# Keys of an attention unit in three chunks of 128 and a shared rest of 64, for every unit instead of for the later ones

## The chip, the cores and the metric

The kernel runs on one core of a Trainium2 chip. The metric is the device time of one execution in microseconds (us); a comparison goes by the median of several. The engines of the core work side by side, each through its own instructions in the order of the program: TensorE (PE; its weight loads are listed as PEld), VectorE (DVE), ScalarE (ACT), GpSimd (POOL) and SyncE (SP). SP and POOL issue the DMA transfers here, and 16 DMA engines carry them out.

## What is computed

The reference is softmax attention, followed by a two-layer network with a leaky ReLU between the layers:

```python
attn = exp(q @ k.T / sqrt(64)); attn /= attn.sum(-1)      # 8 batches, 12 heads, 448 rows, 64 wide
x = (attn @ v).transpose(0, 2, 1, 3).reshape(3584, 768)
h = x @ w_in                                              # 768 x 2048
out = maximum(0.01 * h, h) @ w_out                        # 2048 x 768, float32
```

## The kernel before

**Units.** Attention is worked on in 48 units `u`: batch `u // 6`, and two of its heads. In a unit, `scores(u, c)` (L306) multiplies one chunk of keys by all 448 queries into a PSUM slot, `expo(u, c)` (L321) takes the exponential of it on ACT, `pv` (L361) or `rows` (L857) multiplies the exponentials by the values and by a column of ones, and DVE divides by the sum that the ones give (L873, L874). `x_transposes` (L374) turns the result into `xT`, where the features lie on partitions, on PE (L384) or as a DMA transpose that SP issues (L269).

**Two forms of a unit.** For `u < HY = 18` (batches 0 to 2) the 448 keys are four chunks of 112: eight score matmuls (two heads that lie in the two halves of the partitions), four exponentials of 112x896, and 32 matmuls of 65 columns in `pairs` (L350). For the other 30 units they are three chunks of 128, and the last 64 keys of the two heads share one block of 128 partitions: seven score matmuls, three exponentials of 128x896 and one of 128x448, and in `weighted` (L333) four matmuls of 130 columns and 24 of 65.

**Loads.** `load_soft` (L147) is issued by POOL and casts to bf16 on the way, a transfer for each of q, k, v and each two units; k and v of a later unit take two transfers (L154 to L160). POOL then copies ("casts", L177) each unit's piece into `qkb` (q and k) and `v_old` or `v_sb`; in a later unit the rest of 64 takes two more small copies each for k (L189, L190) and v (L196, L197). q and k are transposed into `qkT` on PE up to unit 14 (L287, `NPE = 15`), then by DMA (L271).

**Order of the work.** The schedule is manual: each engine's order is that of the program. First (L799) come units 0 to 5, one `first(u)` (L761) each, with the casts and loads of later units in `supply(u)` (L749) at hand-set places. `head` (L683) then computes the first layer for the first 448 tokens, `neck` (L702) for the tokens to 640, which belong to batch 1, so it reads `xT` of units 6 to 11. Into these, `place` (L968) puts attention: bursts of three score chunks (L885), `tail` (L901, the score chunk of a rest), transposes, and `rows`, by a small table of assumed durations (`model`, L966) and by the goals `early` and `goals` (L1067); with each burst of head and neck `feed` (L938) issues casts, loads and weight loads. Then `second(i)` (L1031) computes the second layer of token range `i`, with more units placed between the products, and `hidden(i)` (L512) the first layer of the next range, without bursts. `plan` (L965) counts the bursts of each range.

**Stores.** `xT` is a ring of `NX = 15 * 128` tokens (L103). `v_old` lies in the room of `x_mix`, `e_old` in that of the `c` tiles.

Of the kernel before, what the change touches and what calls it, by code (L numbers as in the profile page):

```python
# [16 lines left out]
def kernel(  # L17
# [64 lines left out]
    HY = 3 * HP  # L82
    v_all = v_pool.tile([P, NV, 2 * KC + 2, D + 1], BF16, name="v")
    v_sb = [v_all[:, i] for i in range(NV)]

# [6 lines left out]
    e_old = [c_pool.tile([P, 4 * P], F32, name="c").bitcast(BF16)[:, :2 * S + EP] for _ in range(NE)]  # L92
# [3 lines left out]
    qkT_all = qk_pool.tile([P, NQ, 2, NSC, P], BF16, name="qkT")  # L96
    qkT = [qkT_all[:, i] for i in range(NQ)]
    NB = 3
    qkb_all = cast_pool.tile([P, NB, 2, NSC, 2, D], BF16, name="qkb")
# [3 lines left out]
    NX = 15 * P  # L103

    def place_of(t):
        return (t + NX - cuts[3]) % NX

    OVER = -cuts[3] % S
# [14 lines left out]
    v_old = x_mix.rearrange("p x k n -> p (x k n)")[:SC, :NV * 2 * NSC * (D + 1)].rearrange(  # L123
        "p (u h so d) -> p u h so d", u=NV, h=2, so=NSC)
# [15 lines left out]
    def room(x, new):  # L140

        n = P if x and new else SC
        if not rooms:
            return ld_pool.tile([n, 2, NSC, D], F32, name="f" + "qkv"[x])
        return rooms.pop(0)[:n].bitcast(F32).rearrange("p (h so d) -> p h so d", h=2, so=NSC)

    def load_soft(u, n, which):  # L147
        b, hp = divmod(u, HP)
        hs = slice(2 * hp, 2 * hp + 2 * n)
        for x in which:  # L150
            new = x > 0 and u >= HY
            t = room(x, new).rearrange("p h so d -> p (h so d)").bitcast(BF16)
            t = t.rearrange("p (u h so d) -> p u h so d", u=2, h=2, so=NSC)
            for p, so, keys in ((slice(0, D), NSC, slice(0, NSC * D)), (slice(D, P), KC, slice(NSC * D, S))) if new else (  # L154
                (slice(0, SC), NSC, slice(0, S)),
            ):
                nc.gpsimd.dma_start(  # L157
                    out=t[p, :n, :, :so].rearrange("p u h so d -> p (u h) (so d)"),
                    in_=(q, k, v)[x][b, hs, keys].rearrange("h (p so) d -> p h (so d)", so=so),
                )  # L160
            for i in range(n):
                raw.setdefault(u + i, {})[x] = t[:, i]

    def load_one(u, x, queue):
        b, hp = divmod(u, HP)
        t = room(x, False)
        queue.dma_start(
            out=t.rearrange("p h so d -> p h (so d)"),
            in_=(q, k, v)[x][b, 2 * hp:2 * hp + 2].rearrange("h (p so) d -> p h (so d)", so=NSC),
        )  # L170
        raw.setdefault(u, {})[x] = t

# [4 lines left out]
    def cast(u, parts=(0, 1, 2), by=nc.gpsimd.tensor_copy):  # L177
        if u >= NU:
            return
        for x in parts:  # L180
            f = raw[u].pop(x)
            t = qkb[u % NB]
            if x < 2 and (x == 0 or u < HY):
                by(t[:SC, x].rearrange("p so h d -> p h so d"), f)  # L184
            elif x == 1:
                if u < HY + NB:
                    nc.gpsimd.memset(t[:, 1, KC], 0.0)
                by(t[:, 1, :KC].rearrange("p so h d -> p h so d"), f[:, :, :KC])
                by(t[:D, 1, KC, 0], f[:D, 0, KC])  # L189
                by(t[D:, 1, KC, 1], f[:D, 1, KC])  # L190
            elif u < HY:
                by(v_old[:, u % NV, :, :, :D], f)
            else:
                t = v_sb[u % NV]
                by(t[:, :2 * KC, :D].rearrange("p (h so) d -> p h so d", h=2), f[:, :, :KC])
                by(t[:D, 2 * KC, :D], f[:D, 0, KC])  # L196
                by(t[D:, 2 * KC + 1, :D], f[:D, 1, KC])  # L197
# [17 lines left out]
    make_identity(nc, ident)  # L215
    load_soft(1, 1, (0,))
    load_soft(2, 2, (0, 1))
    load_soft(0, 1, (2,))
    load_soft(1, 2, (2,))
# [5 lines left out]
    warm = h_mix.rearrange("p m c t -> p (m c t)")[:, :512]  # L225
    nc.vector.memset(warm, 0.0)

    gate = const_pool.tile([P, 2], F32)
    nc.vector.memset(gate, 0.0)
# [13 lines left out]
    nc.vector.memset(qkT_all.rearrange("p u i c s -> p u (i c s)")[:, :, 2 * S:2 * S + EP], 0.0)  # L243
    nc.vector.memset(v_old.rearrange("p u h so d -> p (u h so) d")[:, :, D:], 1.0)
    nc.vector.memset(e_all[:SC, :, EM:EM + EP], 0.0)
    for t in e_old:
        nc.vector.memset(t[:SC, 2 * S:], 0.0)
    nc.vector.memset(qkb_all.rearrange("p u i so h d -> p u i (so h d)")[3 * P // 4:, :, 0], 0.0)
    nc.vector.memset(v_all.rearrange("p u c d -> p u (c d)")[:, :, 2 * KC * (D + 1):], 0.0)
    nc.vector.memset(v_all[:, :, :2 * KC, D:], 1.0)  # L250
    for j in range(2):
        nc.vector.memset(v_all[j * D:(j + 1) * D, :, 2 * KC + j, D:], 1.0)
# [17 lines left out]

    def dma_transposes(u):  # L271
        if NPE <= u < HY:
            turn(
                qkT[u % NQ].rearrange("p i c s -> p (i c s)")[:, :2 * S],
                qkb[u % NB][:SC].rearrange("p i so h d -> p (i so h d)"),
            )
        elif NPE <= u < NU:
            nc.sync.dma_start_transpose(
                out=qkT[u % NQ].rearrange("p i c s -> p (i c) s"),
# [850 lines left out]
```

## Time and profile before

| what | us |
|---|---|
| median of 3 runs (382.24 to 384.49) | 382.76 |
| the profiled execution: its span, the one time recorded for it | 381.0 |
| median above that span | 1.8 |
| units 0 to 5, from the first exponential to unit 6's | 7.2 to 26.8 |
| units 6 to 13 with the first layer (head and neck) | about 26.8 to 73.8 |
| second layer of range 0, with its share of units | 73.8 to 105.1 |
| the six further ranges | 105.1 to 381.0 |

The page of the profile gives the busy time of each engine over the span, rows of digits for 40 slices of 9.5 us (9 is busy for 90% or more), groups of instructions with their mean duration, and the chain of work that ended last. The timeline lists instructions by start and duration, in us; rows of a queue (SPq) or rows with DMA are issues, and the trace has for each DMA its issue and its landing. A table by stretches gives busy us of each engine in parts of the span.

### The profile page before, as it was taken

How to read it: one execution, taken by the hardware profiler on the slowest of the kernel's cores; microseconds unless marked ns; L12 is line 12 of the kernel's file. 1: busy time of each engine (PE TensorE's matmuls, PEld its weight loads, DVE VectorE, ACT ScalarE, POOL GpSimd, SP SyncE). 2: the span in 40 equal slices, each digit the busy share in tenths (PEclk: the TensorE clock that was granted, in tenths of full speed). 3: DMA queues.
4: the chain of work that ended last, by engine and by line, in shares of the span. 5: the costliest groups of instructions: out<-in, count | busy, mean ns of one | idle time of the engine just before them, and what ended most of it. 6: DMA issues, size and time to landing. Idle time of an engine off the chain costs nothing.

```text
span 381.0 us, 9888 instructions
## 1 busy us (share of the span) xinstructions
PE 373.0 (98%) x3944; PEld 262.3 (69%) x3944; DVE 229.9 (60%) x488; ACT 254.9 (67%) x391; POOL 183.7 (48%) x376
## 2 busy tenths in 40 slices
PE   7899999999999999999999999999999999999996
PEld 3665657766598656886658866588665895668854
DVE  5663847445766646566476573765736665474753
ACT  5998885765848876478764878638787388617700
POOL 8988820996979456760576603848027100000000
PEclk9999999999999999999999999999999999999999
DMA  9999999699999759991499915999139800330022
GB/s 159 200 201 203 180 191 181 90 170 203 144 168 157 101 102 161 206 129 28 87 172 197 145 28 67 174 202 146 25 68 192 147 14 2 80 109 29 2 82 85
DMA packets 99294, 47.84 MB, mean 126 GB/s; under 512 B 63664, under 2 KB 95920, under 8 KB 99248
## 3 DMA queue, kind: packets, MB, share of 16 engines
q0 software_dynamic: 40384, 22.47, 47.9%
q1 hardware_dynamic: 58608, 24.52, 33.0%
q8 instruction: 31, 0.51, 0.5%
q10 hardware_dynamic: 256, 0.22, 0.2%
q14 instruction: 15, 0.12, 0.1%
HBM read 45.61 MB, written 11.01 MB: 149 GB/s over the span
## 4 chain that ended last, share of the span: by engine, by line
PE 93%; ACT 4%; DMA 1%; issue 1%; DVE 0%; ACTq 0%; DVEq 0%
PE g L609 32%; PE g L537 14%; PE sc L537 14%; PE sc L317 7%; PE sc L345 6%; PE g L419 4%; PE sc L314 4%; PE sc L357 3%; PE g L674 3%; ACT e L326 3%; PE g L715 2%; PE sc L338 2%; PE g L296 1%; DMA w_in_mix<-in_k_dram 1%; PE g L357 1%; ACT c L329 1%
## 5 line engine op out<-in xcount | busy, mean ns | idle before, releaser
L326 ACT ACTIVATE e<-sc 128x896 bf16<-128x896 f32 (+1 forms) x144 | 123.9, 930 | 34.0 <-PE sc L317 20.4
L609 PEld LDWEIGHTS <-h 128*128 128x128 bf16 x632 | 59.3, 98 | 44.7 <-issue 9.3
L609 PE MATMUL g<-w_out_sb,h 128*128 128x384 bf16 x416 | 78.7, 326 | 0.0
L184 POOL COPY qkb<-fq 112x512 bf16<-112x512 bf16 x36 | 24.0, 665 | 90.7 <-DMA qkT<-qkb 74.9
L526 ACT ACTIVATE h<-c 128x512 bf16<-128x512 f32 (+1 forms) x72 | 43.5, 611 | 25.2 <-DVE c L552 15.8
L537 PEld LDWEIGHTS <-w_in_sb 128*128 128x128 bf16 x576 | 54.3, 98 | 5.9
L537 PEld LDWEIGHTS <-w_in_mix 128*128 128x128 bf16 x432 | 41.2, 98 | 4.1
L873 DVE RECIPROCAL rec<-sc 112x8 f32<-112x8 f32 x42 | 8.7, 207 | 54.2 <-PE sc L345 25.9
L609 PE MATMUL g<-w_mix,h 128*128 128x384 bf16 (+1 forms) x208 | 39.0, 323 | 0.0
L614 DVE COPY o<-g 128x384 f32<-128x384 f32 x49 | 27.1, 552 | 10.4 <-PE g L609 10.1
L345 PE MATMUL sc<-v,e 128*128 128x65 bf16 x720 | 33.3, 193 | 0.0
L317 PE MATMUL sc<-qkT 64*128 64x448 bf16 (+1 forms) x210 | 32.8, 352 | 0.0
L345 PEld LDWEIGHTS <-e 128*128 128x128 bf16 x720 | 31.1, 98 | 1.4
L617 DVE TENSOR_TENSOR o<-o,g 128x384 f32<-128x384 f32 x39 | 21.6, 554 | 16.3 <-PE g L609 15.3
L874 DVE TENSOR_TENSOR x<-sc,rec 112x512 bf16<-112x512 f32 x42 | 29.0, 691 | 1.5
L537 PE MATMUL sc<-xT,w_in_sb 128*128 128x256 bf16 (+1 forms) x216 | 28.5, 268 | 0.0
L537 PE MATMUL g<-xT,w_in_sb 128*128 128x256 bf16 (+1 forms) x216 | 28.5, 268 | 0.0
L549 ACT COPY c<-g 128x512 f32<-128x512 f32 (+1 forms) x12 | 6.8, 569 | 30.8 <-PE g L537 30.8
L338 PE MATMUL sc<-v,e 128*128 128x130 bf16 x120 | 26.5, 220 | 0.0
L157 POOL DMA_DIRECT2D fv<-in_v_dram x33 | 20.6, 631 | 4.1 <-POOL v L197 2.4
L314 PE MATMUL sc<-qkT 64*128 64x448 bf16 x144 | 19.9, 357 | 2.1 <-ACT e L326 1.0
L357 PEld LDWEIGHTS <-e 112*128 112x128 bf16 x432 | 20.0, 98 | 1.8 <-issue 0.4
(131 smaller groups left out, 684.0 us busy)
## 6 DMA issues: line engine op xcount, KB each, us to landing
fq<-in_q_dram POOLq DMA_DIRECT2D x18, 224.0 KB, 5.9
w_in_sb<-in_moe_w_in_dram POOLq DMA_DIRECT2D x4, 768.0 KB, 11.2
w_out_sb<-in_moe_w_out_dram POOLq DMA_DIRECT2D x4, 768.0 KB, 19.5
out_dram<-o SPq DMA_DIRECT2D x7, 336.0 KB, 3.4
out_dram<-o SPq DMA_DIRECT2D x8, 288.0 KB, 4.0
fk<-in_k_dram POOLq DMA_DIRECT2D x15, 128.0 KB, 5.7
fv<-in_v_dram POOLq DMA_DIRECT2D x15, 128.0 KB, 4.1
out_dram<-o SPq DMA_DIRECT2D x7, 240.0 KB, 3.4
```

The costliest lines, as they stand in the source:

```text
L184: by(t[:SC, x].rearrange("p so h d -> p h so d"), f)
L314: nc.tensor.matmul(ps[:, j, :S], t[p, S + c * SC:S + c * SC + P], t[p, :S], start=True, stop=True)
L317: nc.tensor.matmul(ps[:, j, :S].rearrange("p (so s) -> p so s", so=NSC), t[p, 1, c], t[p, 0, :, :SC], start=True, stop=True,)
L326: nc.scalar.activation(e[:, :, c, :], ps[:n, :, :S], AX.Exp, scale=scale)
L338: nc.tensor.matmul(ps, e[:, EM + qc * SC:EM + qc * SC + P], vt[:, 2 * KC:].rearrange("p j d -> p (j d)"), start=True, stop=False, skip_gro ...
L345: nc.tensor.matmul(ps[:, j * (D + 1):(j + 1) * (D + 1)], e[:, at:at + P], vt[:, j * KC + c], start=False, stop=(c == KC - 1), skip_group_c ...
L357: nc.tensor.matmul(ps[:, qc, :], t[:SC, at:at + P], vt[:, c], start=(c == 0), stop=(c == NSC - 1),)
L526: nc.scalar.activation(hs[:, m:m + 2, cols], x.rearrange("p (m t) -> p m t", m=2), AX.Prelu, alpha=0.01)
L537: nc.tensor.matmul(ps[:, j * nh:(j + 1) * nh], w[:, kk, ts(j, P)], x[:, kk], start=(first and j == 0 and kk == 0), stop=(kk == KH - 1), sk ...
L609: nc.tensor.matmul(ps[:, cols], x[:, m], w[:, m], start=(first and m == 0), stop=(m == MH - 1), skip_group_check=True,)
L614: by(o[:, at], ps[:, :NW])
L874: nc.vector.tensor_mul(x, ps[:, :, :, :D], rec.to_broadcast([SC, 2, 2 * NP, D]))
```

## The change

All 48 units take the form with three chunks and a rest. The rests of k and of v are no longer loaded with the units: `load_rest(b, x)` loads those of a whole batch (12 heads, 64 keys) in two transfers, one for each half of the partitions, straight into a block-wise store whose other blocks hold zeros. There is room for two batches. The rests of k are transposed on PE with each unit's other pieces for batch 0, and for later batches by one DMA transpose of six blocks on SP, `turn_rest(b)`. `feed` and `advance` call `rests()`, which issues these when units are far enough. The main part is cut like this:

```diff
+    v_rest = v_pool.tile([P, 2, HP, 2, D + 1], BF16, name="vr")
+    k_rest = qk_pool.tile([P, 2, HP, 2, D], BF16, name="kr")
+    kT_rest = qk_pool.tile([P, 2, HP, P], BF16, name="krT")
-    NX = 15 * P
+    NX = 12 * P
...
+    def load_rest(b, x):
+        t = (None, k_rest, v_rest)[x]
+        for j in range(2):
+            nc.gpsimd.dma_start(
+                out=t[j * D:(j + 1) * D, b % 2, :, j, :D],
+                in_=(q, k, v)[x][b, j::2, KS:].rearrange("h p d -> p h d"),
+            )
...
+    nc.vector.memset(k_rest.rearrange("p b u h d -> p (b u h d)"), 0.0)
+    nc.vector.memset(v_rest.rearrange("p b u j d -> p (b u j d)"), 0.0)
     load_soft(1, 1, (0,))
     load_soft(2, 2, (0, 1))
+    load_rest(0, 1)
     load_soft(0, 1, (2,))
+    load_rest(0, 2)
     load_soft(1, 2, (2,))
...
+    def turn_rest(b):
+        nc.sync.dma_start_transpose(out=kT_rest[:, b % 2], in_=k_rest[:, b % 2].rearrange("p u h d -> p (u h d)"))
+    def rest_transpose(u):
+        tr = turn_tile(None)[:, :P]
+        flip(tr, k_rest[:, 0, u], P)
+        nc.vector.tensor_copy(qkT[u % NQ][:, S + KS:], tr)
...
+        ks = kT_rest[:, u // HP % 2, u % HP] if c == KC and u >= HP else t[:, at:at + P]
...
     def supply(u):
-        ... 1: [('qk', 4), ('v', 3), ('load', 8)], ...
+        ... 1: [('qk', 4), ('v', 3), ('rest', 1), ('load', 8)], ...
...
     def first(u):
         if u >= 2:
             x_transposes(u - 2, next_bank())
+        if u == 0:
+            rest_transpose(0)
...
     transposes(HP + 1)
+    turn_rest(1)
     cast(HP + 2, (2,))
     cast(HP + 3)
+    load_rest(2, 1)
-    chunk = NSC * HP + 3
-    nxt = HY
-    owed_t = []
+    nxt = HP + 1
+    owed_t = [HP]
...
+    def rests():
+        full, b = nxt - len(owed_t), to["v rest"]
+        if b < B and rows_done >= HP * (b - 1):
+            load_rest(b, 2)
+            to["v rest"] += 1
+        b = to["k rest"]
+        if b < B and to["rest"] == b and full >= HP * (b - 1):
+            load_rest(b, 1)
+            to["k rest"] += 1
+        b = to["rest"]
+        if b < to["k rest"] and full >= HP * (b - 1) + 2:
+            turn_rest(b)
+            to["rest"] += 1
...
-    plan = [8, 6, 6, 6, 6, 4, 0]
+    plan = [6, 6, 6, 6, 6, 4, 0]
-    early = [1, 2, 4, 6, 7, 9, 11]
-    goals = [1, 4]
+    early = [1, 3, 5, 7, 9, 11]
+    goals = [3]
```

`pairs`, `v_old` and `e_old` go; `pv` takes two blocks of 112 queries at a time for both heads instead of one head for all four. In `cast`, k and v become one copy of 128x384 each. The ring of `xT` is shorter, so that the copy of its overhang (L471) falls to range 2 (192 tokens wide) instead of range 3 (128 wide).

More of the change, by code (lines that the diff above doesn't have):

```diff
@@ L757, in supply @@
                 load(n)
+            elif what == "rest":
+                load_rest(n, 1)
+                load_rest(n, 2)
             else:
@@ L847, in turn_next @@
     def turn_next(i):
-        u, old = to["turn"], chunk < NSC * HY
-        full, last = (chunk // NSC, (chunk + 2) // NSC) if old else (nxt - len(owed_t), nxt)
+        u = to["turn"]
+        full, last = nxt - len(owed_t), nxt
         left = need[min(i + 2, NR)] - rows_done
@@ L885, in burst @@
     def burst(lazy=0):
-        nonlocal nxt, chunk
-        old = chunk < NSC * HY
-        todo = [divmod(chunk + x, NSC) for x in range(3)] if old else [(nxt, c) for c in range(KC)]
-        assert rows_done > todo[-1][0] - NE and turned(todo[-1][0]) and to["v"] > rows_done and not owed_t and not late
+        nonlocal nxt
+        todo = [(nxt, c) for c in range(KC)]
+        assert rows_done > nxt - NE and turned(nxt) and to["v"] > rows_done and not owed_t and not late
         for a, c in todo:
```

255 lines of the change are left out of this document (105 added, 150 removed).

## The prediction

> **What bounds the kernel now.** I read the page first: busy times, then the digits of ACT, POOL and DMA.
>
> ```profile
> PE 373.0 (98%) x3944; PEld 262.3 (69%) x3944; DVE 229.9 (60%) x488; ACT 254.9 (67%) x391; POOL 183.7 (48%) x376
> ACT  5998885765848876478764878638787388617700
> POOL 8988820996979456760576603848027100000000
> DMA  9999999699999759991499915999139800330022
> ```
>
> PE is busy almost throughout, but ACT and POOL are fullest in the first three slices, and the DMA engines are full from the start. So I went on to the table by stretches (busy us; the last two columns are the share of 16 DMA engines, over 1 where packets overlap, and GB/s).
>
> ```profile
> 7.20:26.80 19.60, 17.45 (x280) 11.29 (x277) 12.83 (x35) 19.48 (x24) 17.64 (x29) 1.00 1.38 197
> 26.80:62.70 35.90, 35.20 (x438) 21.36 (x437) 20.35 (x42) 27.43 (x39) 19.82 (x31) 1.00 1.28 190
> 62.70:73.80 11.10, 11.07 (x150) 9.65 (x148) 6.78 (x13) 8.55 (x15) 7.26 (x11) 1.00 0.77 110
> 73.80:105.10 31.30, 31.30 (x334) 18.41 (x332) 19.20 (x43) 21.57 (x27) 26.82 (x48) 1.00 1.28 171
> ```
>
> Units 0 to 5 (to 26.8) are bound by ACT, 19.48 of 19.60 us, with POOL at 17.64 close behind. From then on PE is the bound, without holes. The timeline shows the cycle of the first stage and the places where POOL feeds it:
>
> ```profile
> 16.77 2.64 ACT L326 ACTIVATE e<-sc 112x896 bf16<-112x896 f32 x3
> 17.72 0.62 POOL L184 COPY qkb<-w_in_mix 112x512 bf16<-112x512 bf16 x1
> 18.27 0.62 POOL L184 COPY qkb<-w_mix 112x512 bf16<-112x512 bf16 x1
> 19.16 1.05 ACT L329 ACTIVATE c<-sc 112x896 bf16<-112x896 f32 x1
> 19.96 2.68 ACT L326 ACTIVATE e<-sc 112x896 bf16<-112x896 f32 x3
> 21.37 0.57 PE L296 MATMUL g<-ident,qkb 112*128 112x112 bf16 x8
> ```
>
> A unit takes 3.19 us of ACT. Unit 5's q and k are cast until 18.9, its transposes run at 21.4: 2.5 us in hand. The last view is SP's timeline, with the start of the neck on PE, and the DMA of 50 to 57 us:
>
> ```profile
> 39.36 9.04 SPq L269 DMA_TRANSPOSE xT<-x  x3
> ```
> ```profile
> 62.74 1.98 PE L715 MATMUL g<-xT,w_in_sb 128*128 128x192 bf16 x22
> ```
> ```profile
> q0 software_dynamic: 796, 1.19, 93.2%
> q1 hardware_dynamic: 791, 0.19, 21.7%
> ```
>
> SP issues the transposes of `xT` for units 6, 7, 8 at 39.4, 43.3, 47.2; they land at 49.1, 54.5, 59.1, since SP's queue (q1) gets one packet for each packet of the loads (q0), 113 a us. The neck reads the last at 62.7: 3.7 us in hand. These two margins decide.
>
> **The change part by part.**
>
> *ACT.* A 112x896 exponential starts every 0.81 us; the 128x448 one lasts 551 ns, its start to start about 0.43 by the same overlap. Saved: 0.38 for each of units 0 to 5, 2.3 us where ACT is the bound; later it is not, so nothing.
>
> *PE.* A burst takes 0.67 for three pairs, so four chunks were 0.90; now 0.67 + 0.19 for the rest. 32 weighted matmuls took 1.03, the 28 take 1.01. Saved 0.055 a unit, and 0.05 where a transpose falls to DMA (units 6 to 14): 0.6 in head and neck, 0.4 in range 0's second layer. Units 0 to 5 are not at PE.
>
> *Start.* The new transpose of unit 0's rest stands on PE at 7.9 and needs the rest of k, loaded after k of units 2 and 3 (landed 8.97; about 8.8 with 14% fewer bytes). Cost of one rest transfer of 384 packets of 128 B: loads of 512 B packets land every 1.17 us for 448, of 1024 B every 3.78 for 768, that is 42 and 79 ns a packet, and the line through them gives 14 ns at 128 B, 0.35 us a transfer. By bytes alone it is 0.25; if a packet costs a whole 512 B one, 1.0. I take 0.35, as these two rows are the same queue in the same stage. The rest is there at 9.5. Behind it on PE stand unit 1's transposes, so its scores come at 11.0 instead of 9.0, its first exponential at 11.4 instead of 10.4: +1.0. The two memsets that DVE gains, 0.7 us each by the row of the same size, fit before the first cast at 4.05.
>
> *POOL.* Each rest load is an issue: rows of 256 packets take 0.60 of POOL, of 448 0.69, so 0.66. Four come before the first cast (for batch 0), four in `supply(1)` ahead of unit 5's cast: 5.3 us. Casts of 128x384 start every 0.45 instead of 0.56, and a wait of 0.5 goes: unit 5's cast ends at 22.6 instead of 18.9. Its transposes were at 21.4, and by the ACT cycle of 2.83 with the late start (11.4, 14.3, 17.1, 20.0) would stand at the same 21.4. So PE waits 1.3 and unit 5's first exponential starts at 24.3, not 23.15; unit 6's at 27.5, not 26.8: **+0.7** at the end of the stage, instead of -2.3. If POOL's issues were free it is -1.3, if they cost 0.83 (the 768-packet row) +2.
>
> *Batch 1's rests of k.* They land about 24.2, SP then issues `turn_rest(1)`, 768 packets; by q1's share, beside 1024 B loads, it lands at 31 to 33.5. The rest chunk of unit 6, `tail` in the first gap of head, wants it at about 32: **+0.7** (0 to 2.5).
>
> *SP's queue in head.* By `rests()`, `turn_rest(2)` is issued with burst 8, so on SP it stands after `xT` of unit 6 and ahead of units 7 and 8. It waits for batch 2's rests, which POOL issues after unit 9's cast, at about 37, behind the w_in pieces and loads of units 10 to 13 that are in the queue. The loads were through by about 45; with 14 rest transfers' and turn_rest's packets (2.5) and the rests themselves, it is 49.5. Then three us to the first packet (39.4 to about 43 before), then 768 + 448 + 448 packets at 107 a us (between 84 over all of 43 to 59 us and 113): unit 8's `xT` lands at 68.1. Nothing on SP goes around it. Unit 12's `tail` wants `turn_rest(2)` at about 58 and gets it at 60, and that wait lies within the next: the neck would start at 62.7 + 0.7 + 0.7 - 0.6 = 63.5 and now waits to 68.1: **+4.6**. Ends: 0 when q1 moves 1664 packets in 11 us (151 a us), and +9 at 84 a us, which lands at 72.3.
>
> *Weights.* w_out comes some 3 to 5 us later (64.8 before for its last quarter); DVE waits for it with `w_mix` but that is under the neck's wait; without that cover it costs up to 3.
>
> *Later.* For batches 3 to 7 the rests take 20 POOL issues; 30 go, since k and v of 15 pairs of units now take one transfer each instead of two, and so do the four small copies in each of 30 units. POOL isn't the bound there (88.5 us busy of the last 255.6). Five `turn_rest` stand on SP when landings take 3 to 6 us and the margin is two units, about 8: nothing. The DMA share there is 0.63. Copies of the overhang: 6 of 0.21, about 0.25 now, beside PE: nothing. Either way within 1 us.
>
> Sum: 0.7 + 0.7 - 0.6 + 4.6 - 0.4 = +5.0 on the span of 381.0, so 386.0; the median was 1.8 above that span, so **387.8**.
>
> The Trainium skill ("DMA: Bandwidth & Descriptors", Specifications) says that writes below 512 B are read-modify-write and miss line rate. The trace here doesn't bear it out for 384 B packets, median 49 to 51 ns against 60 for 512 B, as by bytes. By the rule a 128 B packet would gain little over a 512 B one, and the sum would be that of the rival "dear packets" below.
>
> **The rivals.**
>
> *The transposes hide.* If q1 moves 151 a us or more, or the rests land before 45, the neck doesn't wait: 0.7 + 0.7 - 0.6 - 0.4 = +0.4, 383.2. For it: packets of 256 B take 18 ns when alone. Against: 113 a us beside w_out, measured on just these transposes.
>
> *POOL keeps ahead too (not slower).* The place is unit 5's cast. If it ends by 21.4 and nothing waits on DMA, ACT keeps its gain: -2.3 - 1.0 = -3.3, 379.5. It decides at 0.5 us an issue (eight issues, 1.2 us to win); the trace has 0.60 at the least for a transfer of 256 packets. For it: POOL has 2.5 us in hand before.
>
> *Dear packets.* At 1.0 us a rest transfer the twelve before `turn_rest(2)` add 0.65 each, 7.8 us, some 6 of it on the neck: 394. Against: the line above.
>
> *The rests on SP in every batch.* If each of the five later `turn_rest` holds up `xT` by a us, 393 with the forecast. Against: margin of two units.
>
> **How the numbers follow.** Forecast 0.50 (own range 385 to 391), transposes hide 0.23, POOL ahead 0.16, dear packets 0.06, SP in every batch 0.05. One per cent, about what a measurement can tell, is 3.8 us: 379.0 and 386.6. Over it lie four fifths of the forecast and the last two rivals: 0.51. Under it two fifths of "POOL ahead": 0.06. Between: 0.43. The range 379.5 to 391.5 leaves out half of "POOL ahead" and the last two, 0.19.
>
> **What would show it.** Right: unit 5's transposes near 22.7, waiting for POOL; ACT's cycle 2.8; SP's `turn_rest(2)` issued near 49, ahead of two `xT`; PE idle some 4 us before L715's successor. Wrong: SP's third `xT` landing before 63; unit 5's cast before 21.

## The result, and the profile after

The changed kernel takes 401.38 us (median of 4 runs, 400.87 to 401.96); the kernel before took 382.70 beside it (382.24 to 384.49). The ratio is 1.048, 95% interval 1.046 to 1.051: slower by 18.7 us, where +5.0 was forecast. The profiled execution has a span of 399.1 us, 18.1 above the span before. Where executions of one kernel differ much below, only the undisturbed ones are counted.

The page of the changed kernel, with the same rows as before and that of the TensorE clock:

```profile
PE 374.7 (94%) x3845; PEld 262.5 (66%) x3845; DVE 233.6 (59%) x484; ACT 249.6 (63%) x391; POOL 156.8 (39%) x255
PE   6887990999999999999999999989999999999996
ACT  4785980466664787548874687735878468807800
POOL 8988590664748404471053701627114010000000
PEclk9899996899999999999999999999999999999999
DMA  9999999998999935999159971899917820222023
```

PE is busy for about the same time as before (374.7 against 373.0), so the 18 us are idle time. The seventh slice (59.9 to 69.8 us) is a 0 on PE, and the clock has a 6 and an 8 there and in the next. The table by stretches (columns as before; the third from the end is the granted clock) cuts that place out:

```profile
7.87:30.51 22.64, 18.96 (x255) 12.25 (x251) 11.95 (x34) 18.04 (x25) 20.88 (x35) 0.92 1.55 169
30.51:60.60 30.09, 27.68 (x334) 16.86 (x331) 16.00 (x34) 23.50 (x35) 23.05 (x37) 1.00 1.32 187
60.60:70.70 10.10, 0.10 (x2) 0.04 (x2) 0.79 (x2) 0.07 (x1) 0.00 (x0) 0.65 1.19 183
70.70:73.80 3.10, 3.10 (x14) 1.02 (x15) 0.79 (x2) 1.43 (x3) 0.78 (x2) 0.50 1.44 176
80.56:91.81 11.25, 10.59 (x140) 9.50 (x139) 6.42 (x11) 6.58 (x13) 5.29 (x8) 1.00 1.11 125
91.81:121.72 29.91, 29.51 (x278) 17.05 (x275) 20.21 (x43) 18.57 (x25) 18.07 (x28) 1.00 1.08 152
```

Units 0 to 5 were bound by ACT before (19.48 of 19.60 us); now ACT is busy for 18.04 of 22.64. For ten microseconds nothing runs but the DMA engines, and for three more PE runs on half its clock. By the landmarks of the two traces the changed kernel is late by +0.7 at the first exponential (7.18 to 7.87), +3.7 at unit 6's (26.84 to 30.51), +5.2 when PE takes up the head for the third time (32.34 to 37.54, now behind the first `tail`), +17.8 at the start of the neck (62.74 to 80.56), +16.6 at the end of the second layer of range 0 (105.10 to 121.72), and +18.1 at the end. In the list of waits (us in total, times, the longest) the large ones are

```profile
DVE x L893 <- DMA xT<-x: 10.1, 1, 10.1
PE sc L387 <- DVE x L893: 10.0, 1, 10.0
PE sc L330 <- DMA krT<-kr: 2.4, 1, 2.4
POOL w_out_sb L212 <- DMA w_in_sb<-in_moe_w_in_dram: 2.6, 1, 2.6
```

and SP's timeline from 20 to 60 us, where before stood three transposes of `xT` and nothing else, is

```profile
26.05 1.31 SPq L284 DMA_TRANSPOSE krT<-kr  x1
42.44 1.19 SPq L270 DMA_TRANSPOSE xT<-x  x1
53.11 1.27 SPq L284 DMA_TRANSPOSE krT<-kr  x1
54.42 6.05 SPq L270 DMA_TRANSPOSE xT<-x  x2
```

**How the hole arises.** The issue at 53.11 is `turn_rest(2)`. It waited for batch 2's rests of k, which POOL issued at 40.76 and which landed at 53.04. Behind it stand the transposes of units 7 and 8; they land at 69.82 and 72.25, after `turn_rest(2)` at 65.70. It is not the neck that waits, as the forecast had it, but unit 10's product on DVE: its result `x` goes into a tile that unit 7's `x` still occupies (`x_pool` has three), and this is free only when unit 7's transpose has landed:

```profile
59.63 0.21 DVE L892 RECIPROCAL rec<-sc 112x8 f32<-112x8 f32 x1 [0.91 <-PE sc L356]
69.91 0.69 DVE L893 TENSOR_TENSOR x<-sc,rec 112x512 bf16<-112x512 f32 x1 [10.07 <-DMA xT<-x]
70.52 0.58 DVE L315 COPY qkT<-g 128x832 bf16<-128x832 bf16 x1
```

The last row shows what else is held: the copy of the next unit's transposes stands behind the product in DVE's order. On PE the same place reads:

```profile
59.92 0.73 PE L422 MATMUL g<-xT,w_in_sb 128*128 128x448 bf16 x3
70.66 0.56 PE L387 MATMUL sc<-ident,x 112*128 112x112 bf16 x4 [10.01 <-DVE x L893]
71.01 1.33 PE L422 MATMUL g<-xT,w_in_sb 128*128 128x448 bf16 x3
```

Three of these matmuls take 0.73 us ahead of the hole and 1.33 behind it: half the clock, from 63.57 to 73.81, which costs about 1.5 us (half of 3.1).

**How the first stage lost 5.2 us.** The first exponentials of units 1 to 6 come 1.7, 2.4, 2.4, 2.4, 3.9 and 3.7 us later than before. Some rows of the timeline of the changed kernel show where:

```profile
2.23 1.36 DVE L224 MEMSET vr<- 128x1560 bf16 x1 [0.28 <-issue]
10.23 0.22 PE L292 MATMUL g<-ident,kr 128*128 128x128 bf16 x1 [1.13 <-DMA kr<-in_k_dram]
...
19.21 2.53 ACT L340 ACTIVATE e<-sc 128x896 bf16<-128x896 f32 x3 [0.27 <-PE sc L334]
...
21.15 0.66 DVE L315 COPY qkT<-g 128x960 bf16<-128x960 bf16 x1 [0.37 <-PE g L292]
21.87 0.55 PE L334 MATMUL sc<-qkT 64*128 64x448 bf16 x4 [0.26 <-DVE qkT L315]
22.33 2.54 ACT L340 ACTIVATE e<-sc 128x896 bf16<-128x896 f32 x3
```

The memset of `v_rest` takes 1.36 us instead of 0.70, and the casts behind it on DVE are late. Unit 0's rest waits 1.13 us for its load. The clock is at half from 12.37 to 15.78. And the cycle of units 2 to 4 is 3.12 to 3.23 us (19.21 to 22.33 here), hardly below the 3.19 before: the exponentials are 0.4 us shorter, but the scores of the next unit wait for DVE's copy of the transposes, and ACT for the scores. Then PE waits 1.14 us for unit 5's cast at 24.95, and the `tail` of unit 6 waits 2.40 us, up to 37.34, for `turn_rest(1)`.

**Why POOL is late.** POOL's timeline has a kind of wait that was nearly absent before:

```profile
21.28 0.72 POOL L159 DMA_DIRECT2D w_mix<-in_q_dram  x1 [0.46 <-DMA w_in_sb<-in_moe_w_in_dram]
22.44 0.75 POOL L159 DMA_DIRECT2D w_mix<-in_k_dram  x1 [0.44 <-DMA w_mix<-in_q_dram]
...
40.76 1.34 POOL L180 DMA_DIRECT2D kr<-in_k_dram  x2 [1.76 <-DMA w_in_sb<-in_moe_w_in_dram]
43.56 1.31 POOL L180 DMA_DIRECT2D vr<-in_v_dram  x2 [1.47 <-DMA o<-in_k_dram]
...
48.58 0.76 POOL L212 DMA_DIRECT2D w_out_sb<-in_moe_w_out_dram  x1 [2.65 <-DMA w_in_sb<-in_moe_w_in_dram]
```

Counted over the trace, no issue of POOL starts with eight earlier transfers of POOL's under way, and ten issues start 0.28 to 0.33 us after the eighth transfer before them has landed (7.28 behind 7.00, 21.28 behind 20.99, 43.56 behind 43.28, 48.58 behind 48.30; the issue at 40.76 comes 1.0 behind it, so that wait is not all of this kind). In the kernel before there is one such issue:

```profile
8.08 0.85 POOL L209 DMA_DIRECT2D w_in_sb<-in_moe_w_in_dram  x1 [0.21 <-PE g L296]
```

The eighth transfer before it landed at 7.79, though the row names PE. The limit is the program's own. By the trace's records of the instructions, POOL's transfers tell of their landing by eight semaphores in turn (numbers 106 to 113), and each of these issues carries a wait for the semaphore that the eighth transfer before it raises; this is so in all twenty traces of this case. `kernel.py` names no semaphore, so they are given out when the program is built. So a rest transfer, which lands some 0.5 us behind the one before it, also takes one of eight semaphores, and holds it until what was issued ahead of it has been carried. Together with the 2.7 us that four rest issues take of POOL ahead of unit 5's cast, this makes POOL late for what follows: the loads of unit 12 are issued at 34.7 to 36.3, in the kernel before at 30.3 to 31.7.

### The profile page after: what moved, and what is told of

It reads as the page before. It is cut to its first block, busy times and chain, and to the rows that moved or that the text cites. A ratio compares the mean times of both kernels' runs of the same rounds, so it can differ in the third digit from the quotient of the medians.

```text
span 399.1 us, 9530 instructions
## 1 busy us (share of the span) xinstructions
PE 374.7 (94%) x3845; PEld 262.5 (66%) x3845; DVE 233.6 (59%) x484; ACT 249.6 (63%) x391; POOL 156.8 (39%) x255
## 3 DMA queue, kind: packets, MB, share of 16 engines
q1 hardware_dynamic: 60432, 24.84, 34.9%
## 4 chain that ended last, share of the span: by engine, by line
PE 78%; DMA 15%; DVE 3%; POOL 2%; issue 1%; ACT 1%; POOLq 0%; DVEq 0%
PE g L612 25%; PE g L540 13%; PE sc L540 13%; DMA xT<-x 8%; PE sc L356 7%; PE sc L334 6%; PE g L422 4%; DMA krT<-kr 3%; PE g L677 3%; PE sc L349 2%; DMA w_mix<-in_q_dram 2%; PE sc L330 2%; DMA w_in_mix<-in_k_dram 2%; PE g L718 1%; POOL w_mix L159 1%
## 5 line engine op out<-in xcount | busy, mean ns | idle before, releaser
L340 ACT ACTIVATE e<-sc 128x896 bf16<-128x896 f32 x144 | 122.7, 918 | 32.3 <-PE sc L334 31.8
L356 PEld LDWEIGHTS <-e 128*128 128x128 bf16 x1152 | 50.2, 98 | 2.1 <-issue 0.2
L356 PE MATMUL sc<-v,e 128*128 128x65 bf16 x1008 | 46.1, 194 | 0.0
L334 PE MATMUL sc<-qkT 64*128 64x448 bf16 x288 | 38.2, 363 | 1.5 <-DVE qkT L315 1.3
L349 PE MATMUL sc<-vr,e 128*128 128x130 bf16 x168 | 36.7, 218 | 0.2 <-ACT e L342 0.2
L893 DVE TENSOR_TENSOR x<-sc,rec 112x512 bf16<-112x512 f32 x42 | 29.1, 692 | 11.5 <-DMA xT<-x 10.1
L342 ACT ACTIVATE e<-sc 128x448 bf16<-128x448 f32 x48 | 26.5, 552 | 6.2 <-PE sc L330 4.6
L620 DVE TENSOR_TENSOR o<-o,g 128x384 f32<-128x384 f32 x39 | 21.5, 553 | 14.7 <-PE g L612 13.9
L552 ACT COPY c<-g 128x512 f32<-128x512 f32 (+1 forms) x12 | 6.8, 569 | 36.3 <-PE g L540 36.3
L200 POOL COPY v<-fv 128x384 bf16<-128x384 bf16 x36 | 20.6, 580 | 14.3 <-PE sc L356 14.2
L198 POOL COPY qkb<-fk 128x384 bf16<-128x384 bf16 x36 | 20.9, 582 | 11.1 <-DMA fk<-in_k_dram 11.1
```

The lines of the kernel that those rows point to most:

```text
L334: nc.tensor.matmul(to[:, j], ks[p], qs[p], start=True, stop=True)
L340: nc.scalar.activation(e[:, :, c, :], ps[:, :, :S], AX.Exp, scale=scale)
L342: nc.scalar.activation(e[:, EM:EL], ps[:, 0, :S], AX.Exp, scale=scale)
L349: nc.tensor.matmul(ps, e[:, EM + qc * SC:EM + qc * SC + P], v_rest[:, u // HP % 2, u % HP].rearrange("p j d -> p (j d)"), start=True, stop ...
L356: nc.tensor.matmul(ps[:, j * (D + 1):(j + 1) * (D + 1)], e[:, at:at + P], vt[:, j * KC + c], start=False, stop=(c == KC - 1), skip_group_c ...
L620: nc.vector.tensor_add(o[:, at], o[:, at], ps[:, :NW])
```

## The experiments

The theory: POOL gives out the rests' loads late, as it is held up by the added issues and by its eight semaphores; `turn_rest` waits for them at the head of SP's queue; and whatever stands behind it there holds up PE. (Where an expectation speaks of a hole at unit 17's scores, the order of SP's transposes shows unit 16.) The rivals: SP's order alone does it; the volume of the transposes on SP's queue does it, wherever they stand; or the loads' bytes do it. Where no range is given, a time is that of one execution. Two versions that were executed four times lay at 386.0 to 390.5 and at 390.0 to 395.8 us, so single times a few us apart do not rank two versions; the argument goes by the waits in the traces.

**Rests of batches 1 and 2 (to unit 14) transposed on PE**, so that no `turn_rest` stands ahead of `xT`.

```diff
-            end = S + KS if u == 0 or u >= HP else QT
+            end = S + KS if u == 0 else QT
...
-    turn_rest(1)
...
-        if b < to["k rest"] and full >= HP * (b - 1) + 2:
+        if b < to["k rest"] and full >= (2 * HP if b == 2 else HP * (b - 1) + 2):
```

> The changed kernel, with the rests of k of units 6 to 14 transposed on PE with the unit's other pieces, so that SP has no transpose of rests before unit 12 (the one of batch 2, for units 15 to 17, comes behind xT of units 7 and 8). Theory A (the holes of 2.4 us at unit 6's tail and of 10.0 us in head come from the two transposes of rests on SP's queue): both holes go, and with the second the 3 us at half clock behind it: about 399.1 - 2.4 - 10.0 - 1.5 = 385, first score burst of head near 35.5, neck near 67. Theory B (the twelve extra loads by POOL and the DMA volume delay everything, whoever transposes): the hole only moves to a later wait, over 394.

It measured 397.1 us (span 395.3). Both holes are gone, as theory A has it: neck at 67.92 instead of 80.56. But the time lies where theory B had it, for the same thing comes back one batch later:

```profile
86.94 1.46 PE L677 MATMUL g<-w_out_sb,h 128*128 128x384 bf16 x8
95.40 1.30 PE L334 MATMUL sc<-qkT 64*128 64x448 bf16 x6 [7.00 <-DMA qkT<-qkb]
```

`turn_rest(3)` waits on SP for its own load (landed 88.47) and is issued at 88.52, unit 16's q and k, cast since about 86.5, behind it at 89.84; they land at 95.36. The clock is at half from 91.6 to 98.4.

**Four tiles for `x`.**

```diff
-    x_pool = ctx.enter_context(tc.tile_pool(name="x", bufs=3))
+    x_pool = ctx.enter_context(tc.tile_pool(name="x", bufs=4))
```

> The changed kernel with four x tiles instead of three, nothing else. If the hole of 10.0 us at 60.6 is unit 10's product waiting for unit 7's x tile (free only when its transpose has landed, at 69.8), unit 10 passes and the wait moves to unit 11 and to the neck, which needs unit 8's xT (landed 72.3): some 10 us of other work lie before the neck, so the hole shrinks to 2 to 5 us and the time to 391 to 394. If the wait were on the neck's data, as the prediction had it, nothing changes: 399.

393.8 us (span 392.1): as expected. The wait on PE falls from 10.01 to 3.21 us:

```profile
69.25 0.54 PE L387 MATMUL sc<-ident,x 112*128 112x112 bf16 x4 [3.21 <-DVE x L893]
```

It is now unit 11's product that needs unit 7's tile (landed at 68.40). That the x tile was what held PE is shown by this run.

**`turn_rest(2)` behind the transposes of units 7 and 8.**

```diff
-        if b < to["k rest"] and full >= HP * (b - 1) + 2:
+        if b < to["k rest"] and full >= (2 * HP if b == 2 else HP * (b - 1) + 2):
```

> The changed kernel with batch 2's transpose of rests issued behind xT of units 7 and 8 on SP instead of ahead of them. If the order alone makes the hole, it goes and the time is 387 to 389. If it is the volume on SP's queue beside saturated loads (1664 packets in all at about 100 a us, from 53 us on or somewhat before), x tiles come free in time but unit 12's tail, at 59.7, waits for the transpose of rests until 66 to 70 instead: a hole of 6 to 10 us at another wait, 394 to 399.

400.3 us, outside both forecasts. The hole shrinks to 4.01 us and moves to the `tail` of unit 12, which wants the rests themselves:

```profile
70.11 0.56 PE L330 MATMUL sc<-qkT,krT 128*128 128x448 bf16 x1 [4.01 <-DMA krT<-kr]
```

The neck comes 4.3 us earlier (76.22), but later waits (1.34 us at 97.92, and 2.04 at 263.97 with half clock behind it) use most of that up. So SP's order alone is not the cause: with the load as late as before, the transpose that stands last on that queue is late.

**The kernel before, with the twelve rest loads and nothing else** (into `v_all`, read by nobody; the first version had DVE's memsets wait for the loads, 8.5 us of PE at 12.9 us, and tells nothing; the second has the memsets first).

```diff
...
+    def load_rest(b, x):
+        for j in range(2):
+            nc.gpsimd.dma_start(
+                out=v_all[j * D:(j + 1) * D, 2 * (x - 1) + b % 2, :HP, :D],
+                in_=(k, v)[x - 1][b, j::2, 6 * D:].rearrange("h p d -> p h d"),
+            )
...
```

> The kernel before with the twelve rest loads of batches 0 to 2 added at the same places, into a part of a tile that nobody reads until it is written anew (it loads them for nothing; all else is as before). Theory A: POOL is later by eight issues, unit 5's casts come at 23 to 25, PE waits 1 to 4 us there and 0 to 2 in head: 384 to 388. Theory B (the loads by themselves are the main cost): 393 or more.

> The kernel before with the twelve rest loads of batches 0 to 2 added, as in e4_before_loads, but with DVE's memsets of the tile that they land in ahead of them in the program; in e4 those memsets waited for the loads, so the first cast stood until 12.9 and some 8 us of its 9 were that. Theory A: the loads alone cost POOL's issues and some waits: 384 to 387. Theory B: 392.

391.7 us, and 387.4 (span 385.4, +4.4): the loads, with the memsets moved for them, cost most of what the first stage lost, and nearly all of it is there at the head (36.52 against 32.34). No run has the memsets moved without the loads. They do not delay the first exponential, which comes at 6.05 here and at 7.18 before; whether they cost something behind it is not shown.

**The same twelve loads with 6 packets each instead of 384.**

```diff
-                out=v_all[j * D:(j + 1) * D, 2 * (x - 1) + b % 2, :HP, :D],
+                out=v_all[j * D:j * D + 1, 2 * (x - 1) + b % 2, :HP, :D],
...
```

> The kernel before with the twelve added loads of which each moves 6 packets on one partition instead of 384 on 64 (nothing reads them; the memsets come first, as in the run with the whole loads, which had +4.9 us of span). It parts the number of transfers from their bytes. If POOL's issues and the limit on transfers in flight cost it: units 0 to 5 as late as with the whole loads, head's third block near 36, 386 to 388. If the packets of the loads cost it: third block near 33, 383 to 385.

389.2 us (span 387.3), no better than with the whole loads, and even a little beyond what the first theory expected. So the packets are not the cost. What the number of transfers costs shows on POOL and PE in this run:

```profile
22.27 0.72 POOL L157 DMA_DIRECT2D w_mix<-in_q_dram  x1 [1.02 <-DMA w_in_sb<-in_moe_w_in_dram]
23.53 0.72 POOL L157 DMA_DIRECT2D w_mix<-in_k_dram  x1 [0.53 <-DMA w_mix<-in_q_dram]
24.67 0.70 POOL L157 DMA_DIRECT2D w_mix<-in_v_dram  x1 [0.43 <-DMA w_mix<-in_k_dram]
```

```profile
26.05 0.37 PE L306 MATMUL g<-ident,qkb 112*128 112x112 bf16 x4 [3.62 <-POOL qkb L192]
```

Unit 5's cast stands behind four small issues (2.0 us) and three loads that wait for a semaphore (2.0 us), and PE waits 3.62 us for it.

**Batch 2's rests of k loaded early**, right after unit 7's casts; SP's order as in the change.

```diff
-        ... 5: [('qk', 8), ('v', 7), ('w', 1), ('load', 12)] ...
+        ... 5: [('qk', 8), ('v', 7), ('k rest', 2), ('w', 1), ('load', 12)] ...
...
-    load_rest(2, 1)
```

> The changed kernel with one edit: the rests of k of batch 2 are loaded by POOL right after unit 7's casts (about 27 us, their buffer is free since unit 5's transpose) instead of behind the casts of units 8 and 9 (40.76); SP's order stays. Theory A (the load was late: POOL gave it out late and it stood behind eight transfers): it lands near 40 instead of 53.0, the transpose of the rests is issued right behind that of unit 6's x, near 44, and lands near 56; unit 7's x follows near 60, so the hole of 10.0 us at 60.6 falls to 0 to 2, and the half clock behind it goes: 389 to 393. Rival B (SP's queue is simply too slow for one more transpose of 768 packets, wherever it is): unit 7's x still lands at 65 or later, the hole stays at 5 or more: 395 to 399.

The loads land at 41.77 instead of 53.04, and SP's queue runs:

```profile
24.68 1.32 SPq L284 DMA_TRANSPOSE krT<-kr  x1
38.98 1.19 SPq L270 DMA_TRANSPOSE xT<-x  x1
41.83 1.27 SPq L284 DMA_TRANSPOSE krT<-kr  x1
43.69 5.79 SPq L270 DMA_TRANSPOSE xT<-x  x2
```

`turn_rest(2)` lands at 49.58, unit 7's `xT` at 52.87, unit 8's at 58.93. The hole is gone, the neck starts at 66.68, 13.9 us earlier than in the change (3.4 of them already at unit 6's `tail`, see below), with the same transposes in the same order on the same queue. So the hole at 60 us was the late load, and not the volume; the run after the next, which has the wait at unit 6's `tail` again, has no hole there either. But the time is 395.5 us (span 393.7), not 389 to 393: 6.11 us come up at 93.15, with 6.8 us of half clock. There the load of the rests is not late (landed 75.59); `turn_rest(3)` (issued 80.39, landed 91.15) stands ahead of unit 16's q and k (84.38, landed 93.10), whose own k landed only at 83.79. At this place the rival, volume, may have a part. Made together with the fourth x tile it gave 398.6:

> The early load of batch 2's rests of k and four x tiles instead of three. If A holds, the early load alone has emptied the hole, and the fourth tile adds 0 to 1: 388 to 392. If B holds, the fourth tile takes most of what is left: 391 to 394, below the fourth tile alone (393.8) by less than 2.

The x tile adds nothing, as the theory has it, but the total was missed: 4.92 us ahead of unit 16's scores and 2.57 at a cast (43.38).

**The next batch treated as well**: batch 3's rests of k loaded when unit 11 is transposed, and each `turn_rest` from batch 3 on issued two units later.

```diff
-        if b < B and to["rest"] == b and full >= HP * (b - 1):
+        if b < B and (to["pe"] >= 2 * HP if b == 3 else to["rest"] == b and full >= HP * (b - 1)):
...
-        if b < to["k rest"] and full >= HP * (b - 1) + 2:
+        if b < to["k rest"] and full >= HP * (b - 1) + (2 if b == 2 else 4):
```

> The changed kernel with only the order of the loads and transposes of rests altered: batch 2's rests of k loaded right after unit 7's casts (the edit that emptied the hole of 10.0 us before, and left one of 6.1 at unit 17's scores with 6.8 us of half clock), batch 3's loaded as soon as unit 11's transposes are done, and the transposes of batch 3 on issued two units later. If the whole loss behind units 0 to 6 was rests that are loaded late and turned ahead of other transposes: the hole of 6.1 falls under 1 and the half clock there goes, 393.7 of span - 6 - 3 = 384 to 387 of span, 386 to 389 as a time, with what remains against the kernel before (3 to 6) lying ahead of the neck. If the hole only moves on to a later batch again: 390 to 395.

393.9 us (span 392.2): a miss for the first forecast, within the second. No `turn_rest` stands ahead of unit 16 any longer (the third comes at 99.22), and the hole there falls from 6.11 to 3.17; what is left is unit 16's own k, which lands at 86.41, with 7 us of transpose behind it. So late loads alone make a hole there, without any rest in the way. And 2.11 us appear at unit 6's `tail`, although nothing ahead of it differs from the run before. The traces suggest on what that hangs. `turn_rest(1)` and a piece of w_in come up at nearly the same moment, on two queues:

| run | w_in piece issued | `turn_rest(1)` issued | landed |
|---|---|---|---|
| changed kernel | 25.73 | 26.05 | 37.30 |
| four x tiles | 25.08 | 25.70 | 36.51 |
| `turn_rest(2)` later | 25.67 | 26.07 | 36.98 |
| next batch treated | 25.49 | 25.70 | 36.77 |
| rests of k early | 24.84 | 24.68 | 31.68 |
| early, four x tiles | 25.07 | 25.05 | 32.91 |

Ahead of the piece of w_in it takes 7.0 to 7.9 us, behind it 10.8 to 11.2. So some 0.2 us at the issue go with 3 to 4 us at the landing; no run changed this order alone.

**A lighter start**: only batch 0's half of the stores is blanked first, and unit 0's rest is transposed behind unit 1's other pieces. It was tried on the version of the run before:

```diff
...
-        if u == 0:
-            rest_transpose(0)
...
         if u == 0:
+            rest_transpose(0)
             cast(2, (0, 1), fast)
```

> The same with the lighter start: only batch 0's half of the stores of rests is set to zero ahead of the first casts, and unit 0's rest is transposed behind unit 1's other pieces instead of ahead of them. If the start's waits (1.0 and 0.7 us) carry over to the end: 0.5 to 1.5 below the run beside it, 385 to 388. If ACT and DVE take up the difference, as in the earlier run of this start (-0.2): the same within 0.5.

391.9 us in the profiled execution (span 390.1), 2.1 us of span less; two more lay at 394.1 and 394.5, no lower than the run before (ratio to before 1.027, 1.021 to 1.032). So a gain is not shown: these two fit the second forecast, the profiled execution neither. In the profiled one `turn_rest(1)` was out ahead of the piece of w_in (26.30 and 26.51; landed 33.75), so the 2.1 can't be put down to the start.

**A line of versions on the PE form** (rests up to unit 14 on PE). First batch 3's load early:

```diff
...
-        if b < B and to["rest"] == b and full >= HP * (b - 1):
+        if b < B and (to["pe"] >= 2 * HP if b == 3 else to["rest"] == b and full >= HP * (b - 1)):
```

> The run e1_pe_rests with batch 3's rests of k loaded as soon as their place is free (behind unit 11's transposes) instead of behind batch 2's transpose of rests. In e1 the hole in head was gone, but PE then stood 7.0 us at 95.4 for unit 17's transposes, which stood on SP behind batch 3's transpose of rests, and that one waited for its load. Theory A (each hole is a transpose of rests on SP that waits for its load, with xT or qkT behind it): that hole goes too, with the half clock behind it: 386 to 389. Theory B (the DMA volume): another hole of 5 us or more opens: over 392.

390.8 us (span 389.0), between the two forecasts: the hole of 7.0 falls to 1.17. With the lighter start added:

> The run e5_pe_rests_early with a lighter start: only batch 0's half of the two stores is blanked ahead of the first cast, the rest of DVE's memsets come behind unit 1's cast, and unit 0's rest is transposed behind unit 1's transposes instead of ahead of them. By the trace of the changed kernel the memsets cost 0.7 us at the first scores and the wait for the rest's load 1 us at unit 1's first exponential, and the short hole lets the clock fall to half for 3.4 us: unit 1 starts near 10.7 instead of 12.1, and no half clock before 30 us; 1.5 to 2.5 us less than e5.

390.6 us, a miss: the first exponential comes at 6.48 instead of 7.87, but unit 1's still at 12.2, since unit 1's own pieces hold a rest of the same load, which lands at 10.13 (PE goes on at 10.27). A start that is made faster ahead of the same load gains nothing there. The neck does come 1.7 us earlier (66.41), as PE's wait for unit 5's cast falls from 2.11 to 0.25, but 2.26 us then stand ahead of unit 16's scores. Then unit `u + 1`'s transposes ahead of the later scores of unit `u`, and unit 5's casts ahead of batch 1's rests of v:

```diff
+        if u != 1:
+            transposes(u + 1)
         if u > 1:
             scores(u, 2)
             scores(u, 3)
-        if u != 1:
-            transposes(u + 1)
...
```

> The run e7_start with two moves in units 0 to 5: a unit's transposes stand on PE ahead of the scores of its predecessor's last two chunks, and unit 5's casts and the loads that the first stage waits for stand ahead of batch 1's rests of v. If the cycle of 3.12 us in the changed kernel is the chain from these transposes by DVE's copy to the next scores, it falls to ACT's 2.83 (three exponentials at 0.81 and one at 0.43), and PE's wait of 1.1 us for unit 5's cast goes: 2 us less than e7. If the cycle is bound by PE's own work, it stays at 3.1 and only the cast's 1.1 goes.

390.1 us, a miss. The rest of PE's wait for unit 5's cast is gone, but the cycle stays at 3.16 to 3.24: ACT now waits 0.25 us in the middle of a unit (for scores that stand behind the transposes) instead of at its start. The cycle of 2.83 that the forecast had was not reached by this order either. Nine matmuls to keep the clock up while unit 1's pieces wait:

> The run e8_start_cycle with nine matmuls on zeros (512 columns) on PE between unit 1's transposes and the transpose of unit 0's rest, where PE waits about 2 us for a load. If the clock falls to half (9.8 to 16.6 us in e8) because PE stands idle there, it stays at 1.0 and units 1 and 2 take 2.8 to 3.3 us each instead of 4.3 and 3.2, so 1 to 2 us less than e8. If the clock falls for another reason, nothing changes.

392.3 us, a miss that leaves the question open: on PE they stand behind unit 1's transposes, the last of which is unit 1's rest and waits 2.97 us for the load itself, so they run behind the wait that they were to cover, from 10.30 to 14.65, and the clock is at half from 10.98. Later `turn_rest` from batch 3 on:

> The run e8_start_cycle with the transposes of rests of batches 3 to 7 issued two units later, so that on SP they stand behind the transposes of q and k of that time. If the remaining 2.1 us hole at 88.8 (unit 17's scores waiting for qkT) is batch 3's transpose of rests standing ahead of it on SP, it goes: 386 to 388. If it is the landing of the transposes as such, it stays: 390.

387.8 us (span 386.0), as expected: a hole of 2.14 us falls to 0.28. Batch 0's rests as POOL's first loads:

> The run e8_start_cycle with batch 0's rests of k as POOL's first loads instead of its fourth and fifth. They then land near 7 us instead of 10, the transpose of unit 0's rest waits for nothing, the clock stays whole, and unit 1 starts near 10.5 (12.2 in e8), unit 2 near 13.4 (16.5): 2 to 3 us less at the end of the first stage, if nothing else binds; units 2 and 3's q and k land 0.8 us later, which may cost 0.5.

392.5 us, a miss: unit 1's first exponential comes at 11.45 instead of 12.21, the clock still falls to half from 10.07 to 13.48, and the head is taken up 0.9 us earlier (33.55), but 3.69 us appear ahead of unit 16's scores, with 6.8 us of half clock. All of these together:

> All of it: rests on PE for units 6 to 14, batch 3's loads early, a lighter start, the other order in the cycle, batch 0's rests first, later transposes of rests. By theory A what is left over the kernel before is POOL's issues and DVE's late waits, while PE has about 0.5 us less to do: 383 to 386. That it beats the kernel before (382.4) is possible only if the three chunks' 0.3 us a unit come through in the first stage.

387.4 us (386.0 to 390.5), ratio to before 1.013 (1.008 to 1.019), above the 383 to 386 expected. And the fixes on the form with `turn_rest` for batches 1 and 2:

> The rests on DMA from batch 1 on as in the change, with the early load of batch 2's, four x tiles, the lighter start and the earlier transposes and casts in units 0 to 5, batch 3's load earlier and the later transposes of rests from batch 3 on two units later. If A holds and the rest of the losses lie in units 0 to 5 and in the waits of later ranges: 384 to 388, so still not below the kernel before, whose cycle of units 0 to 5 was not beaten; if B: 389 to 393.

390.8 us, ratio 1.026 (1.019 to 1.033): above what theory A gave and within the range of the rival, volume, with 1.78 us at unit 0's rest, 2.15 at unit 6's `tail` (`turn_rest(1)` issued 0.4 us behind the piece of w_in) and 2.08 ahead of unit 16's scores. No version of the change came below the kernel before.

## Why the prediction was right or wrong, step by step

Of the 18.1 us of span 13.1 were not forecast: 3.8 ahead of the point where PE takes up the head for the third time (5.2 against 0.7 + 0.7), 7.8 from there to the end of the second layer of range 0 (11.4 against 4.6 - 0.6 - 0.4), and 1.5 behind it.

- **SP's queue in head: the mechanism right, the size wrong.** `turn_rest(2)` did stand ahead of units 7 and 8, the queue did carry them at about the rate taken (1664 packets of 256 B between 56.9 and 71.8, 111 a us, where 107 were taken), and the price was to be 4.6 us. It was 10.0 and about 1.5 of clock. This is the step that failed most, and two terms of it did. The rests were to land at 49.5 and landed at 53.04: the forecast took the loads ahead of them as through by about 45 in the kernel before, where the last of them landed at 48.87; it did not carry POOL's delay, which it had priced at unit 5's cast, on to those loads (the last now landed at 51.84); and it did not have the program's limit of eight transfers under way (no run parts these two). The run with the early load shows that this term makes or unmakes the hole. And the first to wait was taken to be the neck, for unit 8, from 63.5; it was unit 10's product, for unit 7's tile, from 59.8. The list of who reads a transfer had left out who needs the room of its source; the fourth tile showed it.
- **ACT in units 0 to 5: wrong.** 0.38 us a unit were to be saved. The exponentials did get shorter, but the cycle, 3.19 before, came to 3.12 to 3.23, as ACT and PE wait for DVE's copy of the transposes; another order on PE (the run with 390.1 us) moved that wait and did not end it. "Bound by ACT at 19.48 of 19.60" holds for the kernel before; the next bound lay hardly below it, and the forecast priced the stage as if there were none until unit 5's cast.
- **Start: the wait right, its size too small.** +1.0 was forecast for unit 1's first exponential and +1.7 measured (10.39 to 12.10), as batch 0's rests of k were there at 10.10 and not at 9.5. The 0.7 us at unit 0's first exponential are another matter: the memset of `v_rest` took 1.36 us, where 0.7 was taken for each of the two (that of `k_rest` took 0.70), and it delayed the first casts. They do not add to unit 1's: in the run with the lighter start unit 0's came 1.4 us earlier and unit 1's stayed at 12.2. The half clock from 12.4 to 15.8 (+0.7 at unit 2) was not in the sum at all.
- **POOL and unit 5's cast: right where it was looked at.** PE was to wait 1.3 us and waited 1.14; the cast was to end at 22.6 and ended at 25.3, 1.2 of it in three loads that waited for a semaphore. With the longer cycle of ACT the wait was the same by chance. "POOL keeps ahead" was excluded by this.
- **Batch 1's rests:** landing 31 to 33.5 was forecast, and this is what the runs show in which `turn_rest(1)` is issued first (31.7 to 33.8). In the changed kernel it was issued 0.3 us behind a piece of w_in and landed at 37.3: 2.4 us, near the bound of 2.5.
- **A rest transfer at 0.35 us: the order right, the size too small.** The first twelve land 0.35 to 0.67 us behind the transfer before them, 0.48 on average (four of them at 25.58, 25.96, 26.39 and 26.96). Their packets of 128 B take 32 ns by median, those of 384 B 51 and those of 512 B 60: a byte costs about twice as much in the smallest as in the largest of these, and 51 is more than the 45 that "by bytes" would give. The Trainium skill ("DMA: Bandwidth & Descriptors", Specifications) has transfers below 512 B miss line rate, and in that the trace agrees with it. What the runs exclude is the price of the rival "dear packets": at 1.0 us each they could not land that close, and the loads of 6 packets cost the kernel no less than those of 384.
- **PE: the price of the instructions was right, the saving doesn't show.** From the head to the end of range 0's second layer the loss is 11.4 us, and the hole with its clock explains 11.5; the 1.0 us of saving forecast there does not show; small waits (0.41 at the neck, 0.24 behind it) are two of the places where it can have gone.
- **Later ranges:** within 1 us was forecast, +1.5 measured, 1.2 of it in range 3, where PE waits 1.11 us at 265.5 for DVE, which had waited for an `xT`. Its cause stays open: on SP no `turn_rest` stands near (218.94 and 270.57). Where `turn_rest` was issued later and nothing else altered (387.8 against 390.1 us), a wait of 1.19 us in this range went; in the run with 393.9 us, which has that edit too, 1.05 stand there.
- **The range** missed because the bounds of SP's step (0 to +9) were drawn around the rate of the queue, while what was missing, the delay of the loads behind POOL's eight semaphores and the room for `x`, only adds.

What stays open: how much the clock itself costs in the first stage (in the run with warm matmuls these stood behind the wait), why the cycle of units 0 to 5 does not go below 3.1 us in either order tried, what the waits ahead of unit 16's scores owe to the volume of the transfers, and whether more than eight semaphores would help: the program never has more under way, so no run shows what the queue itself would bear.

## What to carry to other kernels

Before moving small loads into a full stage, count the transfers under way and not only their bytes: in the trace before, look for issues that start a constant time after the landing of the n-th transfer ahead, whatever releaser the row names, and for the semaphore that they wait for. A transfer that waits at the head of an in-order queue delays everything behind it, so put the load that it waits for far ahead of it, and follow for each delayed transfer both its readers and the buffer that its source keeps occupied. When the bound of a stage is shortened, work out the cycle of the next engine first: a full engine says nothing of how much lies below it.

## What the runs showed of the hardware that was not expected

- Issuing a transfer costs POOL little less when it is small: 0.51 us for 6 packets, 0.66 for 384 (two take 1.03 and 1.33).
- A packet of 128 B on POOL's queue takes 32 ns by median, of 384 B 51, of 512 B 60, of 1024 B 98 (trace of the changed kernel).
- The same transpose of 768 packets on SP's queue landed 7.0 to 7.9 us after its issue where it was out up to 0.2 us ahead of a piece of w_in on POOL's queue, and 10.7 to 11.2 where it followed 0.2 to 0.6 us behind it (eight runs).
- PE's granted clock falls to 0.5 in pieces of 3.41 us: three of them from 63.57 to 73.81, around the hole from 60.65 to 70.66, and one from 12.37 to 15.78. The Trainium skill ("TensorE: Matmul & The Clock Gate", Part 1) says that the clock falls after an idle window of about 3.4 us and that the windows run freely. The trace agrees on the length of the pieces, but no window that was idle throughout was needed: between 1.2 us and the fall at 12.37 the longest idle stretch of PE is 1.13 us.
- A memset of 128x1560 bf16 took 1.36 us, one of 128x768 uint32, nearly the same bytes, 0.70.
